# Attention stage of a three-part kernel: another order of the parts of a step, and one rotation of four PSUM banks

## The chip, the cores and the metric

One core of one Trainium2 chip runs the whole program. The metric is the device time of one execution in microseconds (us), the median of several runs.

## The reference

Inputs: q, k, v of 4 batches, 8 heads, 768 positions, 64 channels per head, all float32. Three stages follow one another.

```python
keep = (pos[None, :] < 4) | ((rel >= 0) & (rel < 128))      # 4 sink keys and a window of 128
scores = where(keep, q @ k.T / 8, -1e9); a = softmax(scores); x = a @ v      # heads side by side: 512
theta = x @ w_theta; zr, zi = x * cos(theta), x * sin(theta)
u = x + w_tok_r @ zr + w_tok_i @ zi;  x2 = u + relu(u @ w_ch)
out = (sigmoid(causal_conv5(x2)) * (x2 @ w_val)) @ w_out
```

## The kernel before, in words

The change lies in the first stage, `banded_attention` (L263 to L760). Queries are cut into 24 groups of 128 positions, six to a batch. A query group meets its own 128 keys, the 128 before them and the four sink keys; the first group of a batch has no group before it and no separate sinks, so it has less work. A group has four pairs of heads, and one pair is one step: `for t in range(NT + OT)` (L745) runs 96 steps, and 20 more that drain the pipeline. Several groups are in flight: while step t does the scores of its own pair, it transposes the weights of the pair six steps before, multiplies values of a group ten steps before, and does the theta product of a group twenty steps before.

The order is written out by hand. In each step the loop walks `ORDER` (L21), a list of names. A name is either a part of the step (`parts`, L740), or a queue of postponed pieces of work that `later(kind, steps, f)` filled. What is emitted first stands first in the queue of its engine, and every engine works through its queue strictly in order. `TUNE` (L20) holds the step offsets.

The parts that matter here, for a group g with pairs p0 to p3 (t%4 = 0 to 3):

- `scores` (L418, even steps): TensorE, two pairs at once, into two fixed PSUM tiles `bands` (ps_s, two banks each). A band is free again when `softmax` (L435) of its pair has read it on DVE: `COPY_PREDICATED` L447, then two reductions L449.
- `exp` (ACT L455, then L459): the exponentials with their sums rs. `normalise` (L463, even steps): DVE reciprocal L467, then POOL multiplies a two-pair block (L469) in the next step.
- `turn`, that is `weights_T` (L474, even steps): four transposes on TensorE into ps_t (L480); `tcopy`: ACT copies them out as pc (L484); `cut`: POOL makes the two triangles pp and pc (L491, L493).
- `attend` (L499) and `finish` (L554), at t%4 = 2: 32 (first group: 16) value matmuls L508 into ps_x, then one matmul of the sinks, L558, closes the group; `fcopy` copies ps_x to uT on ACT (L559).
- `sinks` (L517, POOL L524), `sinksT` (L530, TensorE L535 into ps_sk), `scopy` (ACT L541), `slow` (DVE L545), `sink` (POOL L549): they build the operand blk of that sinks' matmul.
- `k`, `q` (L391): transposes of keys and queries for the groups to come (L396), copied by `kcopy` and `qcopy` (L405).
- `split` (ACT L567) and `xl` (POOL L569), `theta` (L574): twelve matmuls L101 to L103 into ps_h; `thcopy` copies them out on ACT (L582).
- `wth`, `range`, `join`, `wturn`, `wcopy`: the weights w_theta, w_tok_r and w_tok_i arrive by DMA (SP's queue) and get rewritten on ACT (L133), POOL (L139) and DVE (L148, L151, L154, L242) between the other work. `keep_warm` (L595) puts idle matmuls into the first steps.

PSUM has eight banks here: four for the bands, one for ps_t, two for ps_m (ps_qk, ps_sk) and one, ps_h, that ps_x, the theta tiles and the warming matmuls share (L269 to L271). In the one bank of ps_h the values of a group can only start when the theta tile ahead of them has been copied out, and theta only when the values ahead of it have been.

After the drain the mixing stage (`mixing`, L843) and the last stage (from L999) follow; neither is edited.

Of the kernel before, what the change touches and what calls it, by code (L numbers as in the profile page):

```python
# [9 lines left out]
F32 = mybir.dt.float32  # L10
# [6 lines left out]
PSUM = bass.MemoryType.PSUM  # L17
DRAM = bass.MemoryType.DRAM

TUNE = dict(tc=0, xs=0, we=0, low=1, cut=1, xl=0, th=0, fx=0, nrm=0, w0=18, ll=8, lv=4, lq=4, lk=5, e=0, l2=0, ws=2, wp=3, ga=0, gc=1, cq=5, ck=5, OT=20, LT=6, OX=10, s1=0, s2=2, sl=1, ss=0, lf=0, rk=0, pcd=0, WP=6, kt=2, bk=3, bq=3, bv=3, bqT=2, first=2, kw=4)  # L20
ORDER = ("range scale warm sinksT cut xl turn scores attend finish wth value wcopy scopy slow tcopy load "  # L21
         "softmax normalise low loads sink exp join sinks k sinkk q split theta qcopy fcopy thcopy fetch kcopy "
         "wturn ").split()

TWO_PI = 6.283185
INV_TWO_PI = 1.0 / (2.0 * math.pi)
# [9 lines left out]
def tile_sink_window_attention__then__token_mix__then__gated_conv(  # L36
# [16 lines left out]
    nc = tc.nc  # L53
    B, H, S, D = q.shape
    P = 128
    NP = H // 2
    NQ = S // P
    DM = H * D
# [24 lines left out]
    wth = [chunks(big.tile([P, KC, DM], F32R, tag=f"wA{z}", name=f"wth{z}")) for z in "hl"]  # L83
    th = {}
# [178 lines left out]
    def banded_attention(mixer):  # L263
        with ExitStack() as c0:
            pa = c0.enter_context(tc.tile_pool(name="pa", bufs=2))
            cq = c0.enter_context(ExitStack())
            pq = cq.enter_context(tc.tile_pool(name="pq", bufs=2, side="right"))
            ps_s = cq.enter_context(tc.tile_pool(name="ps_s", bufs=2, space=PSUM, side="right"))
            ps_t = c0.enter_context(tc.tile_pool(name="ps_t", bufs=1, space=PSUM))  # L269
            ps_m = c0.enter_context(tc.tile_pool(name="ps_m", bufs=2, space=PSUM))  # L270
            ps_h = c0.enter_context(tc.tile_pool(name="ps_h", bufs=1, space=PSUM))  # L271

            ns = max(0, n_sink)
            ns += ns % 2
# [30 lines left out]
            qn, kn, vn, qTs, vss, sms, pTs, sks, blks, xs, pss = ({} for _ in range(11))  # L305
# [85 lines left out]
            def qk_transpose(g, which, p0=0, p1=NP):  # L391
                i = g % NQ
                src = (qn if which == 0 else kn)[g]
                ps = ps_m.tile([P, NP, P], F32, tag="m", name="ps_qk")[:, 0:p1 - p0, :]
                for p in range(p0, p1):
                    nc.tensor.transpose(ps[:, p - p0, :], src[:, 2 * p:2 * p + 2, :].rearrange("s h d -> s (h d)"), ident)  # L396
                if which == 0:
                    if p0 == 0:
                        qTs[g] = pq.tile([P, NP, P], F32, tag="qT", name="qT", bufs=TUNE["bqT"])
                    d = qTs[g][:, p0:p1, :]  # L400
                else:
                    d = kT[:, p0:p1, i, 0:P]

                def copies():
                    copier(which if g == 0 else g < TUNE["ck" if which else "cq"])(d, ps)  # L405
                    if p1 == NP and which == 1 and i == 0 and ns:
# [67 lines left out]
            def weights_T(t):  # L474
                g, p0 = divmod(t, NP)
                i = g % NQ
                sm = sms[g][0]
                ps = ps_t.tile([P, 4, P], F32, tag="t", name="ps_t")
                for n in range(4):
                    nc.tensor.transpose(ps[:, n, :], sm[:, n % 2, p0 + n // 2, ns:], ident)  # L480

                def copy():
                    pc = pa.tile([P, 4, P], F32, tag="pc", name="pc", bufs=3)
                    copier(TUNE['tc'])(pc, ps)  # L484
                    pp = pa.tile([P, 4, P], F32, tag="pp", name="pp", bufs=3) if i > 0 else None
                    pTs[t] = (pc, pp)
                    if i > 0:
                        later("cut", TUNE['cut'], lambda: cut(pc, pp))

                def cut(pc, pp):  # L490
                    nc.gpsimd.affine_select(out=pp, in_=pc, pattern=[[0, 4], [-1, P]], base=0, channel_multiplier=1,  # L491
                                            compare_op=ALU.is_gt, fill=0.0)
                    nc.gpsimd.affine_select(out=pc, in_=pc, pattern=[[0, 4], [1, P]], base=0, channel_multiplier=-1,  # L493
                                            compare_op=ALU.is_ge, fill=0.0)

                later("tcopy", 0, copy)


            def attend(g):  # L499
                i = g % NQ  # L500
                x = xs[g] = ps_h.tile([P, NP, P], F32, tag="h", name="ps_x")
                last = ns == 0 or i == 0
                for p in range(NP):
                    pc, pp = pTs[NP * g + p // 2 * 2]
                    parts = [(g, pc)] if pp is None else [(g, pc), (g - 1, pp)]
                    for a, (gv, w) in enumerate(parts):
                        for h in range(2):
                            nc.tensor.matmul(x[h * D:(h + 1) * D, p, :], vn[gv][:, 2 * p + h, :],  # L508
                                             w[:, p % 2 * 2 + h, :], start=(a == 0 and p == 0),
                                             stop=(last and p == NP - 1 and a == len(parts) - 1),  # L510
                                             skip_group_check=True)
# [18 lines left out]
            def sink_T(g):  # L530
                if ns == 0 or g % NQ == 0:
                    return
                sk = sks.pop(g)
                ps = ps_m.tile([P, NP, P], F32, tag="m", name="ps_sk")[:, 0, :]
                nc.tensor.transpose(ps, sk.rearrange("q a r -> q (a r)"), ident)  # L535
                r = pa.tile([P, P], F32R, tag="skr", name="skr")
                blk = pa.tile([P, NP, P], F32R, tag="blk", name="blk")
                blks[g] = blk

                def copy():  # L540
                    nc.scalar.copy(r, ps)  # L541
                    later("slow", TUNE['sl'], low)

                def low():
                    nc.vector.tensor_tensor(r[64:96, :], ps[64:96, :], r[64:96, :].bitcast(F32), ALU.subtract)  # L545
                    later("sink", TUNE['ss'], block)

                def block():
                    nc.gpsimd.tensor_tensor(blk, r[:, None, :].bitcast(F32).to_broadcast([P, NP, P]),  # L549
                                            bmask[:, :, None].to_broadcast([P, NP, P]), ALU.mult)  # L550

                later("scopy", 0, copy)

            def finish_x(g):  # L554
                b = g // NQ
                x = xs.pop(g)
                if ns and g % NQ:
                    nc.tensor.matmul(x, vss[b], blks.pop(g), start=False, stop=True, skip_group_check=True)  # L558
                later("fcopy", 0, lambda: copier(TUNE['fx'])(uT[:, :, cols(g)], x))  # L559

            def split_x(g):
# [10 lines left out]
            hps = {}  # L572

            def theta(g, c):  # L574
                if c == 0:
                    hps[g] = (ps_m.tile([P, DM], F32, tag="m", name="ps_h") if OT + NP * g > NT - 2 and g % 2 else
                              ps_h.tile([P, DM], F32, tag="h", name="ps_h"))
# [15 lines left out]
            nc.vector.memset(blank, 0.0)  # L593

            def keep_warm(n):  # L595
                warm = ps_h.tile([P, 512], F32, tag="h", name="ps_warm")
# [129 lines left out]
            def step_load_sinks(t, g, p):  # L726
                if ns and g < NG:
# [9 lines left out]
                    if 0 <= n < 6 and b + 1 < B:  # L737
# [398 lines left out]
```

## Time and profile before

| what | value |
|---|---|
| median of 3 runs | 662.92 us (662.25 to 663.28) |
| the profiled execution | 663.22 us; span 661.5 us; mean granted TensorE clock 0.994 |
| busy share of the span | PE 96%, DVE 72%, POOL 60%, ACT 55% |
| attention stage | from 0 to about 235 us, 24 groups; values of group 2 start at 46.89, of group 6 at 84.42, of group 12 at 138.70, of group 18 at 192.97 |
| instructions | 12467 |

The span is counted from the first to the last instruction; the execution's own time is 1.7 us longer. A group of rows by line shows how often an instruction ran, its mean time and what ended the idle time before it; a row of the timeline gives the start, the length and, in brackets, the idle time just before it. Matmuls overlap, so the distance from one start to the next is their price on TensorE, not the length in the row.

### The profile page before, as it was taken

How to read it: one execution, taken by the hardware profiler on the slowest of the kernel's cores; microseconds unless marked ns; L12 is line 12 of the kernel's file. 1: busy time of each engine (PE TensorE's matmuls, PEld its weight loads, DVE VectorE, ACT ScalarE, POOL GpSimd, SP SyncE). 2: the span in 40 equal slices, each digit the busy share in tenths (PEclk: the TensorE clock that was granted, in tenths of full speed). 3: DMA queues.
4: the chain of work that ended last, by engine and by line, in shares of the span. 5: the costliest groups of instructions: out<-in, count | busy, mean ns of one | idle time of the engine just before them, and what ended most of it. 6: DMA issues, size and time to landing. Idle time of an engine off the chain costs nothing.

```text
span 661.5 us, 12467 instructions
## 1 busy us (share of the span) xinstructions
PE 635.8 (96%) x4454; PEld 566.9 (86%) x4454; DVE 477.6 (72%) x1187; ACT 362.1 (55%) x1013; POOL 396.8 (60%) x406
## 2 busy tenths in 40 slices
PE   8679999999999999999999999999999999999998
PEld 4457777777877789999999999999989989989997
DVE  4876677777688449546756767766979889889773
ACT  4779898898898776534353444452423333323222
POOL 4699899879969864324343344447836637537330
PEclk9889999999999999999999999999999999999999
DMA  7686697799982460001000010110010110110111
GB/s 165 162 186 144 139 210 156 147 202 177 199 166 59 137 206 3 1 16 49 33 33 32 33 50 33 49 47 2 1 48 1 49 48 1 49 48 1 49 48 49
DMA packets 104335, 53.36 MB, mean 81 GB/s; under 512 B 80593, under 2 KB 96209, under 8 KB 104273
## 3 DMA queue, kind: packets, MB, share of 16 engines
q1 hardware_dynamic: 104272, 52.56, 32.7%
q8 instruction: 35, 0.57, 0.4%
q14 instruction: 28, 0.22, 0.1%
HBM read 41.54 MB, written 11.01 MB: 79 GB/s over the span
## 4 chain that ended last, share of the span: by engine, by line
PE 69%; POOL 13%; DVE 7%; ACT 5%; issue 3%; DMA 2%; SPq 0%; ACTq 0%; POOLq 0%; DVEq 0%
PE ps_y L103 10%; PE ps_y L101 10%; PE ps_y L102 10%; PE ps_x L508 4%; PE ps_o L103 3%; POOL sm L469 3%; DVE acc L1047 3%; PE ps_o L102 3%; PE ps_o L101 3%; PE ps_c L103 3%; PE ps_c L102 3%; PE ps_c L101 3%; POOL pc L493 2%; PE ps_v L101 2%; PE ps_v L102 2%
## 5 line engine op out<-in xcount | busy, mean ns | idle before, releaser
L98 POOL TENSOR_TENSOR zl<-cs,zh 128x512 fp32r<-128x512 f32 x48 | 65.9, 1373 | 95.2 <-ACT zh L97 80.1
L1047 DVE SCALAR_TENSOR_TENSOR acc<-x,cw,acc 128x384 f32<-128x384 f32 x128 | 106.6, 833 | 2.4
L455 ACT ACTIVATE sm<-sm,nm 128x132 f32<-128x132 f32 (+1 forms) x192 | 76.3, 403 | 13.1 <-DVE nm L449 12.6
L98 POOL TENSOR_TENSOR x2l<-x,x2h 128x384 fp32r<-128x384 f32 x32 | 39.3, 1227 | 55.3 <-ACT x2h L97 55.3
L97 ACT CAST zh<-cs 128x512 fp32r<-128x512 f32 x48 | 29.9, 622 | 76.8 <-DVE cs L892 66.5
L101 PE MATMUL ps_y<-wt0h,zh 128*128 128x384 f32 x192 | 68.2, 355 | 0.0
L469 POOL TENSOR_TENSOR sm<-sm,rs 128x512 f32<-128x512 f32 x48 | 55.9, 1164 | 20.3 <-DVE rs L467 12.7
L103 PE MATMUL ps_y<-wt1h,zl 128*128 128x384 f32 x192 | 64.6, 336 | 0.0
L102 PE MATMUL ps_y<-wt1l,zh 128*128 128x384 f32 x192 | 64.5, 336 | 0.0
L103 PE MATMUL ps_y<-wt0h,zl 128*128 128x384 f32 x192 | 64.5, 336 | 0.0
L102 PE MATMUL ps_y<-wt0l,zh 128*128 128x384 f32 x192 | 64.4, 336 | 0.0
L101 PE MATMUL ps_y<-wt1h,zh 128*128 128x384 f32 x192 | 64.4, 336 | 0.0
L447 DVE COPY_PREDICATED ps_s<-upper,ps_s 128x256 f32<-128x256 int32 x80 | 33.7, 422 | 36.8 <-PE ps_s L432 36.3
L449 DVE CUSTOM_DVE_ANT_0 sm<-ps_s,mask 128x132 f32<-128x132 f32 (+1 forms) x192 | 48.9, 291 | 12.2 <-PE ps_s L424 7.4
L98 POOL TENSOR_TENSOR gl<-acc,gh 128x384 fp32r<-128x384 f32 x28 | 33.7, 1204 | 22.4 <-ACT gh L97 22.4
L508 PE MATMUL ps_x<-pc,vn 128*64 128x128 f32 x384 | 38.0, 286 | 8.8 <-ACT th L582 4.3
L97 ACT CAST x2h<-x 128x384 fp32r<-128x384 f32 x32 | 16.4, 513 | 54.7 <-DVE x L1033 54.7
L101 PE MATMUL ps_v<-x2h,held 128*128 128x384 f32 x128 | 43.3, 338 | 0.0
L102 PE MATMUL ps_v<-x2l,held 128*128 128x384 f32 x128 | 43.2, 338 | 0.0
L103 PE MATMUL ps_v<-x2h,held 128*128 128x384 f32 x128 | 43.2, 338 | 0.0
L892 DVE TENSOR_TENSOR cs<-cs,ps_n 128x512 f32<-128x512 f32 x48 | 32.7, 681 | 11.6 <-ACT cs L885 10.2
L432 PE MATMUL ps_s<-kT,qT 64*64 64x196 f32 x640 | 38.3, 350 | 2.6 <-DVE nm L449 2.2
(159 smaller groups left out, 1937.9 us busy)
## 6 DMA issues: line engine op xcount, KB each, us to landing
vn<-in_v_dram SPq DMA_DIRECT2D x24, 256.0 KB
kn<-in_k_dram SPq DMA_DIRECT2D x23, 256.0 KB
qn<-in_q_dram SPq DMA_DIRECT2D x23, 256.0 KB
out_dram<-o SPq DMA_DIRECT2D x23, 256.0 KB
late<-in_moe_w_tok_r_dram SPq DMA_DIRECT2D x24, 192.0 KB
late<-in_moe_w_tok_i_dram SPq DMA_DIRECT2D x24, 192.0 KB
wTr<-wTe SPq DMA_DIRECT2D x24, 96.0 KB
wTi<-wTe SPq DMA_DIRECT2D x24, 96.0 KB
```

The source lines that it names most:

```text
L97: nc.scalar.copy(dst_h, src)
L98: lo_engine.tensor_tensor(dst_l, src, dst_h.bitcast(F32), ALU.subtract)
L101: nc.tensor.matmul(ps, lhs[0], rhs[0], start=first, stop=False)
L102: nc.tensor.matmul(ps, lhs[0], rhs[1], start=False, stop=False)
L103: nc.tensor.matmul(ps, lhs[1], rhs[0], start=False, stop=last)
L432: nc.tensor.matmul(ps[a:a + QW, h, a:KT + a + QW], qTs[g][d, p, a:a + QW], keys[:, a:KT + a + QW], start=True, stop=True)
L447: nc.vector.copy_predicated(ps[:, :, KT:KT + P], upper.bitcast(I32)[:, None, :].to_broadcast([P, 2, P]), ps[:, :, 0:P])
L449: nc.vector.tensor_tensor_reduce(sm[:, h, p, a:], ps[:, h, P:KT + P - a], m, -SCALE, BIG, ALU.add, ALU.min, nm[:, h, p:p + 1])
L455: nc.scalar.activation(x, x, AF.Exp, bias=nm[:, h, p:p + 1], scale=-1.0, accum_out=rs[:, h, p:p + 1])
L469: later("scale", 0, lambda: nc.gpsimd.tensor_tensor(x, x, r[:, :, :, None].to_broadcast([P, 2, 2, P]), ALU.mult))
L508: nc.tensor.matmul(x[h * D:(h + 1) * D, p, :], vn[gv][:, 2 * p + h, :], w[:, p % 2 * 2 + h, :], start=(a == 0 and p == 0), stop=(last and ...
L1047: nc.vector.scalar_tensor_tensor(a, x2[:, e, z:z + TB], cw[:, e, z:z + 1], a, ALU.mult, ALU.add)
```

## The change

Four edits.

1. `ORDER` is another permutation of the same names. `scores` now stands ahead of `turn` and `attend`; `sinksT` behind `attend`; `tcopy`, `scopy` and `thcopy` ahead of `exp`; `cut` first on POOL; `join` ahead of `normalise`; `wth` and `split` behind `thcopy`; `wcopy` ahead of `load`.
2. Offsets: `s2` 2 to 3 (the sinks' transpose one step later), `lq` 4 to 3 (queries' transposes one step later), `low` 1 to 2, `l2` 0 to 1, `kt` 2 to 4, `cq` 5 to 6 and `ck` 5 to 4 (which of the early q and k copies run on DVE).
3. The sinks' matmul opens the group of the values instead of closing it.
4. The pools ps_t, ps_m and ps_h become one pool of four banks. Every tile that is not of the scores (ps_t, ps_qk, ps_sk, ps_x, ps_h, the warming tile) takes the next bank in turn, so it waits for the readers of the tile four allocations before it.

```diff
-TUNE = dict(tc=0, xs=0, we=0, low=1, ... lq=4, lk=5, e=0, l2=0, ... cq=5, ck=5, ... s2=2, ... kt=2, ...)
-ORDER = ("range scale warm sinksT cut xl turn scores attend finish wth value wcopy scopy slow tcopy load "
-         "softmax normalise low loads sink exp join sinks k sinkk q split theta qcopy fcopy thcopy fetch kcopy "
-         "wturn ").split()
+TUNE = dict(tc=0, xs=0, we=0, low=2, ... lq=3, lk=5, e=0, l2=1, ... cq=6, ck=4, ... s2=3, ... kt=4, ...)
+ORDER = ("warm cut range slow scale xl scores sink turn tcopy attend wcopy sinksT softmax theta load scopy "
+         "finish join normalise k thcopy sinkk wth loads split exp wturn sinks low q fcopy value qcopy kcopy "
+         "fetch").split()
...
-            ps_t = c0.enter_context(tc.tile_pool(name="ps_t", bufs=1, space=PSUM))
-            ps_m = c0.enter_context(tc.tile_pool(name="ps_m", bufs=2, space=PSUM))
-            ps_h = c0.enter_context(tc.tile_pool(name="ps_h", bufs=1, space=PSUM))
+            psum = c0.enter_context(tc.tile_pool(name="psum", bufs=4, space=PSUM))
+
+            def bank(shape, name):
+                return psum.tile(shape, F32, tag="b", name=name)
...
-                x = xs[g] = ps_h.tile([P, NP, P], F32, tag="h", name="ps_x")
-                last = ns == 0 or i == 0
+                x = xs[g] = bank([P, NP, P], "ps_x")
+                sinks = ns > 0 and i > 0
+                if sinks:
+                    nc.tensor.matmul(x, vss[g // NQ], blks.pop(g), start=True, stop=False, skip_group_check=True)
...
-                if ns and g % NQ:
-                    nc.tensor.matmul(x, vss[b], blks.pop(g), start=False, stop=True, skip_group_check=True)
```

How the queues change at the places of which the prediction speaks:

TensorE in the steady state, from the end of a group's theta product to the first value matmuls of the next group's values; ps_s_93 and ps_s_94 are the two bands (ps_s_87 and ps_s_88 in the change). Before:

```order
L103 MATMUL ps_h<-wthh,xl 128x512
L535 MATMUL ps_sk<-ident,sk 128x128
L480 MATMUL ps_t<-ident,sm 128x128 x4
L432 MATMUL ps_s_93<-kT,qT 64x196 x4
L432 MATMUL ps_s_94<-kT,qT 64x196 x4
L508 MATMUL ps_x<-pc,vn 64x128 x2
```

With the change:

```order
L103 MATMUL ps_h<-wthh,xl 128x512
L398 MATMUL ps_qk<-ident,qn 128x128 x4
L434 MATMUL ps_s_87<-kT,qT 64x196 x4
L434 MATMUL ps_s_88<-kT,qT 64x196 x4
L482 MATMUL ps_t<-ident,sm 128x128 x4
L506 MATMUL ps_x<-blk,vr 128x512
L512 MATMUL ps_x<-pc,vn 64x128 x2
```

The queries' transposes came between theta and the scores, the sinks' transpose left this place, the weights' transposes follow the scores, and the sinks' matmul opens the values.

ACT over the same stretch and on to the copy of ps_x. Before:

```order
L567 CAST xh<-uT 128x512
L405 COPY qT<-ps_qk 128x512
L455 ACTIVATE sm,rs<-sm,nm 128x132 x2
L459 ACTIVATE rs<-rs,eps 128x2x2
L582 COPY th_791<-ps_h 128x512
L541 CAST skr<-ps_sk 128x128
L484 COPY pc<-ps_t 128x512
L455 ACTIVATE sm,rs<-sm,nm 128x132 x2
L559 COPY uT<-ps_x 128x4x128
```

With the change:

```order
L568 CAST xh<-uT 128x512
L457 ACTIVATE sm,rs<-sm,nm 128x132 x2
L582 COPY th_774<-ps_h 128x512
L457 ACTIVATE sm,rs<-sm,nm 128x132 x2
L461 ACTIVATE rs<-rs,eps 128x2x2
L407 COPY qT<-ps_qk 128x512
L486 COPY pc<-ps_t 128x512
L457 ACTIVATE sm,rs<-sm,nm 128x132 x2
L560 COPY uT<-ps_x 128x4x128
L545 CAST skr<-ps_sk 128x128
```

The copy of the theta tile moved ahead of the exponentials of the same step, the copy of the queries behind them, and the sinks' copy behind that of ps_x.

TensorE in the start-up, around the transposes of the second group's sinks. Before:

```order
L598 MATMUL ps_warm<-blank 128x512
L535 MATMUL ps_sk<-ident,sk 128x128
L480 MATMUL ps_t<-ident,sm 128x128 x4
L432 MATMUL ps_s_93<-kT,qT 64x196 x4
L432 MATMUL ps_s_94<-kT,qT 64x196 x4
L508 MATMUL ps_x<-pc,vn 64x128 x8
```

With the change:

```order
L434 MATMUL ps_s_87<-kT,qT 64x196 x4
L434 MATMUL ps_s_88<-kT,qT 64x196 x4
L482 MATMUL ps_t<-ident,sm 128x128 x4
L512 MATMUL ps_x<-pc,vn 64x128 x8
L539 MATMUL ps_sk<-ident,sk 128x128
L398 MATMUL ps_qk<-ident,kn 128x128 x4
```

The sinks' transpose stood ahead of the weights' transposes, the scores and the values of its step, and now stands behind all three.

## Rows read from the trace of the kernel before

**Rows 1.** Busy time by stretch: us, then each engine, granted clock, DMA

```profile
84.42:138.70 54.28, 51.67 (x530) 40.67 (x530) 40.24 (x157) 48.34 (x163) 48.01 (x53) 1.00 0.85 175
...
232.72:661.50 428.78, 424.83 (x2383) 406.66 (x2383) 313.50 (x560) 170.15 (x369) 201.80 (x168) 1.00 0.11 38
```

**Rows 2.** Waits of TensorE, 47 to 240 us: total, times, longest

```profile
PE ps_x L508 <- ACT th L582: 4.3, 9, 0.9
PE ps_x L508 <- issue: 2.2, 2, 1.2
PE ps_x L508 <- POOL xl L569: 1.9, 2, 0.9
```

**Rows 3.** Waits of TensorE, 0 to 47 us

```profile
PE ps_sk L535 <- POOL sk L524: 5.4, 3, 2.2
...
PE ps_t L480 <- ACT pc L484: 1.4, 1, 1.4
```

**Rows 4.** Timeline of TensorE: start, length, instruction, idle time before it

```profile
102.47 0.39 PE L508 MATMUL ps_x<-pc,vn 128*64 128x128 f32 x4
102.69 0.39 PE L508 MATMUL ps_x<-pp,vn 128*64 128x128 f32 x4
103.00 0.50 PE L558 MATMUL ps_x<-blk,vr 128*128 128x512 f32 x1
103.34 0.60 PE L396 MATMUL ps_qk<-ident,kn 128*128 128x128 f32 x4
103.78 0.60 PE L480 MATMUL ps_t<-ident,sm 128*128 128x128 f32 x4
...
108.53 0.40 PE L103 MATMUL ps_h<-wthh,xl 128*128 128x512 f32 x1
...
108.87 0.60 PE L480 MATMUL ps_t<-ident,sm 128*128 128x128 f32 x4
109.40 0.89 PE L432 MATMUL ps_s<-kT,qT 64*64 64x196 f32 x16
111.23 0.44 PE L508 MATMUL ps_x<-pc,vn 128*64 128x128 f32 x4 [0.94 <-ACT th L582]
...
122.92 0.89 PE L432 MATMUL ps_s<-kT,qT 64*64 64x196 f32 x16
123.74 0.65 PE L396 MATMUL ps_qk<-ident,qn 128*128 128x128 f32 x4
```

**Rows 5.** Timeline of ACT, the same group

```profile
109.48 0.42 ACT L455 ACTIVATE sm<-sm,nm 128x132 f32<-128x132 f32 x1
...
110.61 0.57 ACT L582 COPY th<-ps_h 128x512 f32<-128x512 f32 x1
```

**Rows 6.** Timeline of DVE, three places

```profile
101.91 1.68 DVE L154 SCALAR_TENSOR_TENSOR wc<-late,wc 128x768 int32<-128x768 int32 x1
...
110.03 0.43 DVE L447 COPY_PREDICATED ps_s<-upper,ps_s 128x256 f32<-128x256 int32 x1 [2.11 <-PE ps_s L432]
...
111.02 1.10 DVE L148 TENSOR_SCALAR wc<-wc 128x768 int32<-128x768 int32 x1
...
127.72 1.75 DVE L151 SCALAR_TENSOR_TENSOR wc<-late,wc 128x768 int32<-128x768 int32 x1
```

**Rows 7.** Timeline of POOL in the start-up

```profile
23.91 1.27 POOL L98 TENSOR_TENSOR wthl<-wc,wthh 128x512 fp32r<-128x512 f32 x1 [2.03 <-ACT wthh L97]
...
29.30 1.33 POOL L469 TENSOR_TENSOR sm<-sm,rs 128x512 f32<-128x512 f32 x1 [1.41 <-DVE rs L467]
...
42.23 1.27 POOL L98 TENSOR_TENSOR wthl<-wc,wthh 128x512 fp32r<-128x512 f32 x1 [1.23 <-ACT wthh L97]
...
47.59 1.28 POOL L569 TENSOR_TENSOR xl<-uT,xh 128x512 fp32r<-128x512 f32 x1
```

**Rows 8.** Waits of POOL, 84 to 193 us

```profile
POOL sm L469 <- DVE rs L467: 6.4, 4, 1.9
POOL sk L524 <- DVE rs L467: 4.5, 2, 2.3
```

More of the change, by code (lines that the diff above doesn't have):

```diff
@@ L18 @@
 DRAM = bass.MemoryType.DRAM
-TUNE = dict(tc=0, xs=0, we=0, low=1, cut=1, xl=0, th=0, fx=0, nrm=0, w0=18, ll=8, lv=4, lq=4, lk=5, e=0, l2=0, ws=2, wp=3, ga=0, gc=1, cq=5, ck=5, OT=20, LT=6, OX=10, s1=0, s2=2, sl=1, ss=0, lf=0, rk=0, pcd=0, WP=6, kt=2, bk=3, bq=3, bv=3, bqT=2, first=2, kw=4)
-ORDER = ("range scale warm sinksT cut xl turn scores attend finish wth value wcopy scopy slow tcopy load "
-         "softmax normalise low loads sink exp join sinks k sinkk q split theta qcopy fcopy thcopy fetch kcopy "
-         "wturn ").split()
+TUNE = dict(tc=0, xs=0, we=0, low=2, cut=1, xl=0, th=0, fx=0, nrm=0, w0=18, ll=8, lv=4, lq=3, lk=5, e=0, l2=1, ws=2, wp=3, ga=0, gc=1, cq=6, ck=4, OT=20, LT=6, OX=10, s1=0, s2=3, sl=1, ss=0, lf=0, rk=0, pcd=0, WP=6, kt=4, bk=3, bq=3, bv=3, bqT=2, first=2, kw=4)
+ORDER = ("warm cut range slow scale xl scores sink turn tcopy attend wcopy sinksT softmax theta load scopy "
+         "finish join normalise k thcopy sinkk wth loads split exp wturn sinks low q fcopy value qcopy kcopy "
+         "fetch").split()
 TWO_PI = 6.283185
@@ L393, in qk_transpose @@
                 src = (qn if which == 0 else kn)[g]
-                ps = ps_m.tile([P, NP, P], F32, tag="m", name="ps_qk")[:, 0:p1 - p0, :]
+                ps = bank([P, NP, P], "ps_qk")[:, 0:p1 - p0, :]
                 for p in range(p0, p1):
@@ L477, in weights_T @@
                 sm = sms[g][0]
-                ps = ps_t.tile([P, 4, P], F32, tag="t", name="ps_t")
+                ps = bank([P, 4, P], "ps_t")
                 for n in range(4):
@@ L508, in attend @@
                             nc.tensor.matmul(x[h * D:(h + 1) * D, p, :], vn[gv][:, 2 * p + h, :],
-                                             w[:, p % 2 * 2 + h, :], start=(a == 0 and p == 0),
-                                             stop=(last and p == NP - 1 and a == len(parts) - 1),
+                                             w[:, p % 2 * 2 + h, :], start=(not sinks and a == 0 and p == 0),
+                                             stop=(p == NP - 1 and a == len(parts) - 1),
                                              skip_group_check=True)
@@ L533, in sink_T @@
                 sk = sks.pop(g)
-                ps = ps_m.tile([P, NP, P], F32, tag="m", name="ps_sk")[:, 0, :]
+                ps = bank([P, NP, P], "ps_sk")[:, 0, :]
                 nc.tensor.transpose(ps, sk.rearrange("q a r -> q (a r)"), ident)
@@ L554, in finish_x @@
             def finish_x(g):
-                b = g // NQ
                 x = xs.pop(g)
-                if ns and g % NQ:
-                    nc.tensor.matmul(x, vss[b], blks.pop(g), start=False, stop=True, skip_group_check=True)
                 later("fcopy", 0, lambda: copier(TUNE['fx'])(uT[:, :, cols(g)], x))
@@ L575, in theta @@
                 if c == 0:
-                    hps[g] = (ps_m.tile([P, DM], F32, tag="m", name="ps_h") if OT + NP * g > NT - 2 and g % 2 else
-                              ps_h.tile([P, DM], F32, tag="h", name="ps_h"))
+                    hps[g] = bank([P, DM], "ps_h")
                 x2 = xs[g, "hl"]
@@ L595, in keep_warm @@
             def keep_warm(n):
-                warm = ps_h.tile([P, 512], F32, tag="h", name="ps_warm")
+                warm = bank([P, 512], "ps_warm")
                 for _ in range(n):
```

## The prediction

> **What bounds the kernel now.** I read the busy time by stretch first, to see which engine each stage is full of. From group 6 to group 12, one batch, TensorE is busy 51.67 of 54.28 us [rows 1]; POOL has 48.01 and ACT 48.34, so they have 6 us of room in a batch and TensorE 2.6. From 232.72 us to the end TensorE is busy 424.83 of 428.78 us [rows 1]: nothing in the change touches that stretch, and I leave it as it is. What can be won lies in TensorE's waits of the first 235 us, and the second view lists them.
>
> From 47 to 240 us thirteen waits stand at one instruction, the first value matmul: 4.3 us released by the theta copy on ACT, 2.2 with no releaser and 1.9 put down to POOL, 8.4 together [rows 2]. Two timelines show why. The last theta matmul starts at 108.53, transposes and scores follow at 108.87 and 109.40, and the values start at 111.23, behind an idle 0.94 [rows 4]. ACT was doing the exponentials of p1 from 109.48 and came to the theta copy only at 110.61; it took 0.57 and ended 0.05 before the values started [rows 5]. Values and theta share one bank, and the copy that frees it stands behind exponentials. That a part of the 8.4 us has another name I put down to the same bank, since it is the same instruction with the same length of wait; if not, the 4.3 us are the lower end.
>
> In the first 47 us TensorE waits 5.4 us in three waits for POOL's sinks' weights, with transposes and scores queued behind, and 1.4 us for the single ps_t bank [rows 3].
>
> **The change part by part.** The sum is made against the profiled execution of 663.2 us, which lies 0.3 above the median shown.
>
> *Banks in turn, theta's copy ahead of the exponentials.* A steady group now takes seven tiles in this order: transposes, theta, queries, transposes, values, sinks, keys. Four back from the values lies the first transposes' tile, copied long before; theta's tile is now awaited by the sinks' transpose, 4 us of TensorE work later. So all thirteen waits go: -8.4 us (at least -4.3). In exchange theta waits for the copy of ps_x, as it did before. ACT, in order, now stands idle at the theta copy until theta ends, about 1 us a group. That costs nothing as long as ACT has room: 54.28 less 48.34 is 5.9 us a batch, 1.0 a group [rows 1]. If it had none, the exponentials would be late, then the reciprocal, then POOL; their results are wanted only one to two steps later.
>
> *Order on TensorE.* No instruction is added or removed. By distances from start to start the price of most blocks stays: scores followed by transposes 0.82 (122.92 to 123.74), four transposes 0.44 (103.34 to 103.78), the sinks' matmul 0.34 (103.00 to 103.34) [rows 4]. Where the array's shape changes (the third field, 128\*64, 64\*64, 128\*128) there is an extra: 0.53 instead of 0.44 for transposes ahead of scores (108.87 to 109.40), 0.31 instead of 0.22 from the last values to the sinks (102.69 to 103.00) [rows 4]. A full group had five such changes and now has six, because scores sit between two blocks of transposes and the sinks' matmul no longer follows the values. The price is 0.09 in 20 groups, +1.8 us; the ends are 0 (the block left may have paid it already) and 3.2 (0.50 of the sinks' length less its 0.34 distance, the whole overlap lost, 20 times [rows 4]). The Trainium skill, TensorEngine Tiling (Array Packing), section Key Properties, says that changing the tiling mode drains TensorE, which speaks against an order with one more change; by it the term would be the upper end and the time 1.4 us longer, and the 0.09 of the rows shows much less than an empty engine.
>
> *Scores first.* A band is filled again sooner. From the scores of p2 and p3 to the second half of the next scores TensorE has 0.82 + 0.44 + 0.34 + 1.85 (seven distances of 0.22 and one 0.31) + 0.11 (one transpose, a quarter of 0.44) + 0.53 + 0.41 (the first half of the scores) = 4.50 us of work. DVE needs 0.63 until it starts (109.40 to 110.03), 0.99 for softmax and reciprocal (to 111.02), a piece of the weights' work of 1.10, and 0.90 for the second softmax (0.99 less a short reciprocal): 3.62; with a piece of 1.68 it is 4.20 [rows 4, 6]. Both fit, with 0.3 us to spare. They don't where DVE comes late: behind a piece of 1.75 in the step before [rows 6] I reckon 0.7 late, and 0.4 us of wait. The weights' jobs come every one and a half groups and every second one has its pieces in those steps: 6 groups, +2.4 us, between 0 and the rival below.
>
> *Start-up.* The three waits for the sinks' weights no longer hold up scores, since the sinks' transpose stands behind them and a step later; the copy of ps_t no longer waits for a weights' piece whose DMA is late, and has another bank anyhow. The most is 5.4 + 1.4 = 6.8 us [rows 3]. What is late next is POOL: from 23.91 to 47.59 it is idle only 1.41 + 1.23 = 2.6 us [rows 7]. So the stretch can shrink by that, plus what the first of these rows starts earlier; it waited 2.03 for ACT, and I take 1.6 of it. Together -4.2 us, ends 0 and -6.8.
>
> *With no price of their own.* The sinks' matmul is only moved, but now needs blk at the start of the values instead of the end; blk is made two steps ahead, so TensorE's 3 us of earlier work cover it. `cut` first and `join` ahead of the reciprocal change when POOL waits, not how much it does; what that could cost is the first rival. Of the early copies one goes from ACT to DVE and one back. On SP the stores of the turned weights go ahead of a step's loads; loads are issued eight steps before use, so a store that waits some 2 us for DVE stays hidden.
>
> The sum: -8.4 + 1.8 + 2.4 - 4.2 = -8.4, hence 654.8 against the profiled execution and 654.5 us as a median.
>
> **The rivals.** *POOL becomes the bound.* In two batches POOL waits 6.4 + 4.5 us for the reciprocal [rows 8], 5.5 a batch; with its 48.01 of work that is 53.5 of 54.28. If these waits stay, and they may, because up to 1.75 us of weights' work now stands ahead of the reciprocal, a batch shrinks by 0.8 only. Three batches give -2.4, the start-up nothing: 660.5. For it: POOL has the least room after TensorE. Against: those waits are there because POOL had caught up with a slower TensorE, and shrink as it is asked for more. Chance 0.14.
>
> *The wait moves to theta.* Theta still needs the copy of ps_x, and from the last value matmul to theta TensorE now has 0.11 + 0.53 + 0.82 + 0.44 = 1.9 us of work where it had 0.34 + 0.44 + 0.53 + 0.82 + 0.41 = 2.5. If ACT is behind by 1.4 us there (the copy itself is 0.5), the bank wait is back under another name: -8.4 falls away, the other terms cancel, and the time is 663. For it: ACT is the most filled after TensorE and POOL in rows 1. Against: in the new order it idles for theta once in each group, which absorbs lateness. Chance 0.10.
>
> *The bands become the bound, and it is slower.* If DVE needs not 4.20 but 5.3 us between the two scores, because pieces of 1.7 us stand in both steps, every group loses 0.8 at the scores: 20 times, +16 in place of +2.4, and 668. The turning point is 0.54 us a group (10.8 us over 20 groups), that is 5.04 us on DVE against the 4.50 that TensorE leaves. For it: the pieces reach 1.68 and 1.75 [rows 6]. Against: DVE has 14 us of room in a batch [rows 1], and the sinks' small correction left that interval. Chance 0.12.
>
> **How the numbers follow.** The forecast has 0.64. The lower end of the range, 648.5, is the forecast with terms two and three at nothing and 6 us from the start-up; the upper, 662, takes in the POOL case and half of what the bands may add. About 0.06 lies below and 0.14 above. A measurement of this kernel can tell about 0.2%, 1.3 us. Faster by more: the forecast, most of the POOL case (0.11) and 0.02 of theta's, 0.77. Within: 0.03 and 0.06, 0.09. Slower: the bands and 0.02 of theta's case, 0.14.
>
> **What would show it.** Right: no wait at the first value matmul or at the sinks' opening one; a batch near 51.5 to 52.5 us between the same values of groups 6 and 12; the values of group 2 (46.9 us before) some 4 us earlier; ACT idle ahead of the theta copy, released by TensorE. Each step is wrong if its sign is missing: waits of theta's first matmul for the copy of ps_x, waits of the scores for DVE of more than 0.4 us in most groups, or waits for POOL ahead of the transposes or in the values. The whole is wrong if the stretch after the attention stage changes its length by more than 1 us.

## The result and the profile after

| | median | spread | ratio to the kernel before, 95% interval |
|---|---|---|---|
| before | 662.66 us | 662.25 to 663.28, 4 runs | |
| with the change | 653.52 us | 653.26 to 654.30, 4 runs | 0.9863 (0.9846 to 0.9880) |

The change is faster by 9.1 us, 1.4%. The profiled executions give 661.5 and 652.0 us of span, 9.5 less. The prediction was 654.5 in a range of 648.5 to 662.

By stretch, in the changed kernel (us, then each engine's busy time, granted clock, DMA); the cuts are the first value matmuls of groups 3, 6, 12 and 18 and the first `ps_y` matmul of the mixing stage:

```profile
55.55:82.29 26.74, 26.20 (x266) 20.43 (x265) 19.36 (x74) 24.12 (x82) 25.05 (x27) 1.00 0.70 145
82.29:134.27 51.98, 51.98 (x532) 40.35 (x531) 38.51 (x155) 48.21 (x163) 48.90 (x53) 1.00 0.89 184
...
186.25:234.17 47.92, 47.79 (x438) 37.64 (x437) 31.34 (x102) 39.63 (x116) 43.05 (x46) 1.00 0.57 153
234.17:652.00 417.83, 413.88 (x2313) 397.59 (x2311) 308.16 (x554) 163.65 (x357) 194.39 (x164) 1.00 0.09 32
```

The same stretches that [rows 1] don't have, of the kernel before:

```profile
56.28:84.42 28.14, 26.54 (x265) 20.74 (x265) 19.60 (x76) 24.02 (x82) 24.54 (x26) 1.00 0.73 151
192.97:243.70 50.73, 48.12 (x435) 37.84 (x436) 32.24 (x104) 39.31 (x115) 42.98 (x45) 1.00 0.52 143
243.70:661.50 417.80, 413.85 (x2313) 397.62 (x2311) 308.35 (x554) 163.61 (x357) 194.65 (x165) 1.00 0.09 32
```

A batch took 54.28 us and takes 51.98, and now TensorE is busy in all of it. Up to group 6 the kernel is 2.13 us ahead, each of two batches adds 2.3, the end of the attention stage 2.81, and the untouched rest differs by 0.03.

TensorE's waits from 47 to 240 us, all that are left of the 9.7 that stood there (thirteen at the values, [rows 2], and 1.3 us of others):

```profile
PE ps_s L434 <- DVE nm L451: 0.5, 1, 0.5
```

And in the first 47 us, where [rows 3] stood before:

```profile
PE ps_s L434 <- DVE nm L451: 5.9, 5, 3.5
...
PE ps_x L506 <- POOL blk L553: 0.5, 1, 0.5
```

The waits for the sinks' weights are gone; in their place the scores wait for DVE, 5.9 us in five pieces, where one such wait of 1.5 us stood before. A full group in the middle of the stage shows the dense case (TensorE, then ACT). It answers to [rows 4, 5]:

```profile
105.68 0.40 PE L103 MATMUL ps_h<-wthh,xl 128*128 128x512 f32 x1
105.92 0.60 PE L398 MATMUL ps_qk<-ident,qn 128*128 128x128 f32 x4
106.45 0.90 PE L434 MATMUL ps_s<-kT,qT 64*64 64x196 f32 x16
107.27 0.66 PE L482 MATMUL ps_t<-ident,sm 128*128 128x128 f32 x4
107.69 0.48 PE L506 MATMUL ps_x<-blk,vr 128*128 128x512 f32 x1
108.10 0.44 PE L512 MATMUL ps_x<-pc,vn 128*64 128x128 f32 x4
```

```profile
106.12 0.59 ACT L582 COPY th<-ps_h 128x512 f32<-128x512 f32 x1
106.60 0.41 ACT L457 ACTIVATE sm<-sm,nm 128x132 f32<-128x132 f32 x1
```

No row has an idle time in brackets. Theta's copy starts 0.44 after the start of theta's last matmul and is done at 106.71, a microsecond before the values' group opens. ACT now stands and waits for theta, and for the values (its waits from 84 to 193 us):

```profile
ACT th L582 <- PE ps_h L103: 3.9, 9, 0.6
ACT uT L560 <- PE ps_x L512: 3.0, 6, 0.6
```

### The profile page after: what moved, and what is told of

Its sections match the earlier page's. It is cut to its first block, busy times and chain, and to the rows that moved or that the text cites. A ratio compares the mean times of both kernels' runs of the same rounds, so it can differ in the third digit from the quotient of the medians.

```text
span 652.0 us, 12510 instructions
## 1 busy us (share of the span) xinstructions
PE 636.7 (98%) x4452; PEld 565.5 (87%) x4454; DVE 471.3 (72%) x1187; ACT 362.1 (56%) x1013; POOL 398.5 (61%) x406
## 4 chain that ended last, share of the span: by engine, by line
PE 79%; POOL 8%; DVE 7%; issue 2%; DMA 2%; SPq 1%; ACT 1%; DVEq 0%; POOLq 0%
PE ps_y L103 10%; PE ps_y L101 10%; PE ps_y L102 10%; PE ps_x L512 4%; PE ps_s L434 4%; PE ps_o L103 3%; DVE acc L1047 3%; PE ps_o L101 3%; PE ps_o L102 3%; PE ps_t L482 3%; PE ps_h L102 3%; PE ps_h L103 3%; PE ps_h L101 3%; PE ps_c L101 3%; PE ps_c L103 3%; PE ps_c L102 3%
## 5 line engine op out<-in xcount | busy, mean ns | idle before, releaser
L471 POOL TENSOR_TENSOR sm<-sm,rs 128x512 f32<-128x512 f32 x48 | 53.8, 1120 | 8.9 <-DVE rs L469 8.9
L892 DVE TENSOR_TENSOR cs<-cs,ps_n 128x512 f32<-128x512 f32 x48 | 32.7, 682 | 10.9 <-ACT cs L885 10.9
L101 PE MATMUL ps_h<-wthh,xh 128*128 128x512 f32 x96 | 39.8, 415 | 0.0
```

Of the source, the lines that this page charges most:

```text
L101: nc.tensor.matmul(ps, lhs[0], rhs[0], start=first, stop=False)
L471: later("scale", 0, lambda: nc.gpsimd.tensor_tensor(x, x, r[:, :, :, None].to_broadcast([P, 2, 2, P]), ALU.mult))
L892: nc.vector.tensor_tensor(x, x, pn[:, None, :].to_broadcast([P, 2, HD]), ALU.mult)
```

## The experiments

Each was run beside the kernel before on the same chip, in five rounds. "g3" to "g18" is the start of the values of that group in the profile, "mix" the first matmul of the mixing stage. Before and after stand there for comparison. The kernel before took 663.2 to 663.3 us in these runs and 662.7 beside the changed kernel, so medians of the two sets can be compared to about 0.6 us.

| kernel | median us | ratio (95%) | g3 | g6 | g12 | g18 | mix | span |
|---|---|---|---|---|---|---|---|---|
| before | 662.66 | | 56.28 | 84.42 | 138.70 | 192.97 | 243.70 | 661.5 |
| changed | 653.52 | 0.985 to 0.988 | 55.55 | 82.29 | 134.27 | 186.25 | 234.17 | 652.0 |
| rot_only | 656.94 | 0.989 to 0.992 | 56.05 | 81.93 | 134.42 | 186.90 | 237.06 | 654.9 |
| order_only | 656.23 | 0.988 to 0.991 | 53.99 | 81.87 | 133.93 | 186.01 | 236.59 | 654.4 |
| old_pools | 656.23 | 0.989 to 0.992 | 55.64 | 81.99 | 133.97 | 185.96 | 236.26 | 654.1 |
| theta_copy_only | 674.01 | 1.015 to 1.018 | 56.05 | 86.10 | 144.22 | 202.55 | 254.27 | 672.1 |
| exp_behind | 665.00 | 1.002 to 1.004 | 57.86 | 85.04 | 139.12 | 192.80 | 245.25 | 663.0 |
| five_changes | 652.11 | 0.982 to 0.985 | 53.16 | 80.48 | 132.32 | 184.12 | 232.81 | 650.6 |
| sinks_last | 653.57 | 0.984 to 0.987 | 52.98 | 80.87 | 132.92 | 184.99 | 233.26 | 651.0 |
| weights_later | 655.46 | 0.987 to 0.990 | 56.48 | 83.83 | 135.81 | 187.79 | 235.71 | 653.5 |
| sinks_turn_early | 658.00 | 0.991 to 0.995 | 60.20 | 86.40 | 138.86 | 191.32 | 240.44 | 658.3 |
| double_fold | 672.69 | 1.014 to 1.016 | 60.94 | 89.00 | 146.13 | 203.26 | 254.53 | 672.3 |
| fetch_early | 650.77 | 0.980 to 0.983 | 51.17 | 79.04 | 130.99 | 182.95 | 230.85 | 648.6 |
| five_fetch | 650.66 | 0.980 to 0.983 | 51.36 | 78.68 | 130.52 | 182.35 | 231.03 | 648.8 |

### Which edit takes the waits at the values away

**rot_only**, the kernel before with the rotation of four banks and nothing else:

```diff
-            ps_t, ps_m, ps_h: pools of 1, 2 and 1 bank
+            psum = c0.enter_context(tc.tile_pool(name="psum", bufs=4, space=PSUM))
```

> The kernel before with the fourth edit alone: one rotation of four banks, the old order of a step, the sinks' matmul last. Theory (the bank is the cause, and the rotation cures it): the values' bank is the one of the queries' transposes, copied long before, so the thirteen waits at the values go (8.4 us) and there is no added change of the array's shape: 653 to 655 us. Rival (the place of theta's copy behind the exponentials is the cause, whatever the bank): the waits stay or move to the next tile, 660 to 663 us.

**order_only**, the new `ORDER` and `TUNE` (edits 1 and 2) with the old pools and the sinks' matmul last:

> The new order and offsets alone (edits 1 and 2), the old pools, the sinks' matmul last. Theory (the order alone takes the waits at the values away, 1.8 us of TensorE work cover theta's copy): 653 to 656 us. Rival (theta and values in one bank: what was waited for at the values is waited for at theta, which has 1.9 us for the copy of ps_x): 658 to 663 us, with waits of L101 for the copy of ps_x.

**old_pools**, the changed kernel with edit 4 undone:

> The changed kernel with the fourth edit undone: three pools again, the new order, the sinks' matmul first. If the rotation is needed, waits come back at theta or at the sinks' matmul that opens the values: 657 to 663 us. If the order alone did it: within 1.5 us of the changed kernel, 652 to 655 us.

Either half does it: the waits for theta's copy are gone in the middle of the stage in all three runs. The rotation alone takes a batch from 54.28 to 52.49 us, the order alone to 52.06, and the new order with the old pools and with the sinks' matmul first to 51.98, the changed kernel's own length. So in the middle of the stage the rotation adds nothing to the order. All three medians lie above what was expected of a cure (655, 656 and 655 us at most); a wait in rot_only and the end of the stage, both below, are why. The Trainium skill, Perfetto Trace Analysis, section Matmuls, says that independent groups should rotate through PSUM banks so that the copy of one overlaps the matmuls of the next; rot_only agrees (6 us), and order_only shows that another order, in which the copy stands ahead of the exponentials, does the same with one bank. In rot_only TensorE has new waits, all at the first transposes of keys in a batch; the profile puts two of them down to ACT (first row) and one to the keys' transfer (second row):

```profile
PE ps_qk L398 <- ACT sm L457: 1.9, 2, 1.2
PE ps_qk L398 <- DMA kn<-in_k_dram: 1.2, 1, 1.2
```

All three look like the transfer. Theta's copy, which frees the bank that these transposes take next, was done at 135.20, a microsecond before the transposes at 136.26 (SP's queue, ACT and TensorE in rot_only), and likewise at 187.68 before those at 189.15. The keys' transfer had gone out at 130.50 and 182.99, 5.8 and 6.2 us before TensorE went on, against 5.7 (78.50 to 84.17) for the wait that bears its name:

```profile
130.50 0.58 SPq L365 DMA_DIRECT2D kn<-in_k_dram  x1
```

```profile
134.63 0.57 ACT L583 COPY th<-ps_h 128x512 f32<-128x512 f32 x1
```

```profile
136.26 0.63 PE L398 MATMUL ps_qk<-ident,kn 128*128 128x128 f32 x4 [0.75 <-ACT sm L457]
```

What the two edits do only together lies at the end of the stage. From group 18 to the mixing stage the old pools need 50.3 to 50.6 us, the rotation with the old order 50.16, both together 47.92. With the old pools the last group's values still wait for theta in the one bank. Scores have run out, so TensorE has no other work between them, and theta's copy comes late because ACT does cosines of the mixing stage first, with 1.28 us for a table (TensorE, then ACT in old_pools):

```profile
225.16 0.47 PE L503 MATMUL ps_x<-blk,vr 128*128 128x512 f32 x1 [1.92 <-ACT th L580]
```

```profile
222.43 1.28 ACT L882 ACT_TABLE_LOAD   x1
...
224.45 0.56 ACT L580 COPY th<-ps_h 128x512 f32<-128x512 f32 x1
```

In order_only the same wait, 1.88 at 225.60, is listed with no releaser.

**theta_copy_only** and **exp_behind**, both the kernel before with one name of the order moved:

```diff
-         "... normalise low loads sink exp join sinks k sinkk q split theta qcopy fcopy thcopy fetch kcopy "
+theta_copy_only: "... normalise low loads sink thcopy exp join sinks k sinkk q split theta qcopy fcopy fetch kcopy "
+exp_behind:      "... normalise low loads sink join sinks k sinkk q split theta qcopy fcopy thcopy exp fetch kcopy "
```

> The kernel before with one name of the order moved: theta's copy ahead of the exponentials on ACT; the old pools. Theory (either half of the step is enough): theta ends near 108.9 in the group of rows 4, the copy takes 0.57 and is done before TensorE has finished transposes and scores (110.3), so the waits at the values go: 654 to 656 us. Rival (exponentials behind an idle ACT are late and hold something else, or only the rotation cures it): 659 to 664 us.

The edit did the opposite of what its expectation says. `theta` stands behind in the walk, so a queue of copies that is emptied before it finds nothing, and the copy goes out a step later. The waits grew, which makes the run a test from the other side: the later the copy, the longer the values wait, 21.6 us in these two rows (the first two of TensorE's waits from 47 us on).

```profile
PE ps_x L508 <- ACT th L582: 16.1, 16, 1.5
PE ps_x L508 <- issue: 5.5, 4, 1.4
```

> The kernel before with one name of the order moved, this time the exponentials: behind theta's copy of the same step; old pools, TensorE's order as before. Theory (theta's copy stood behind exponentials, and one bank joins theta and values): the copy ends 0.6 after theta and TensorE has 1.4 us of transposes and scores in between, so the waits at the values go, without an added change of the array's shape: 653 to 656 us. Rival (exponentials that come last on ACT delay the reciprocal, and POOL or the transposes wait): 658 to 666 us.

Here the copy does come before the exponentials, and the waits at the values for theta's bank shrink to 1.2 us at the last group and 0.2 at another; one for POOL's triangles pc grew from 0.4 to 1.0. Yet nothing is won, 665.0 us. TensorE's waits from 47 us on:

```profile
PE ps_qk L396 <- DMA kn<-in_k_dram: 3.2, 3, 1.3
PE ps_s L432 <- DVE nm L449: 3.0, 5, 0.7
PE ps_x L508 <- issue: 1.2, 1, 1.2
PE ps_x L508 <- POOL pc L493: 1.0, 1, 1.0
```

and in the start-up those for the sinks' weights grew from 5.4 to 7.2 us. The rival was right that the cost moves, though not to POOL alone: the batch is back at 54.08 us with other names at the waits. Taking one wait away was not enough; the order as a whole took its successors away too. In this run the keys' transfer goes out at 82.11, behind four weight loads, and TensorE stands for it until 87.44, as in rot_only. In the changed kernel it goes out at 77.83 and its transposes start at 83.48 without a wait, hardly later; no run tests what keeps the new order clear of it.

### What the shape changes and the third edit cost

**five_changes** and **sinks_last**:

```diff
-ORDER = ("... xl scores sink turn tcopy attend wcopy ... load scopy finish join ...")
+sinks_last:   "... xl scores sink turn tcopy attend finish wcopy ... load scopy join ..."   and the sinks' matmul in finish_x, as before
+five_changes: "... xl sink turn scores tcopy attend finish wcopy ... load scopy join ..."   and the same
```

> The changed kernel with the scores behind the weights' transposes again and the sinks' matmul last: five changes of the array's shape in a full group in place of six; offsets, rotation and ACT's order as changed. Theory (a change of shape costs 0.09 to 0.11, all of it on the path): 20 groups by that, 1.8 to 2.2 us less than the changed kernel, 651.3 to 652.0 us, and a batch of about 51.4 us. Rival (the scores have to go first, or DVE or the values wait): 653.5 to 657 us with waits of the scores for DVE.

> The changed kernel with the third edit undone: the sinks' matmul closes the values again. Theory (six changes of shape either way, and the operand has time enough): 653.0 to 654.5 us, a batch of 52.0. Rival (opening the values with a whole-bank matmul is what saved time): 655 to 657 us.

Full groups without any wait last 8.89 and 8.90 us in the changed kernel (values at 90.31, 99.20, 108.10) and 8.83 and 8.82 in five_changes (88.15, 96.98, 105.80): one change of the array's shape less is worth 0.07 us a group. The batch shrinks by 0.14 only, since some scores stall on DVE (0.16 at 123.11). The 1.4 us by which the median is lower come from the start-up, 1.8 at group 6, less 0.8 that the end gives back. sinks_last shows the same start-up gain (group 3 2.6 us sooner) without the lower number of changes, keeps 1.4 of it at group 6 and 0.9 at the mixing stage, and its median equals the changed kernel's. In neither run is this gain a wait less. Up to group 3 TensorE is idle for 10.97 us in five_changes and 10.60 in sinks_last, and for 10.70 in the changed kernel; it is busy for 42.19 and 42.38 in place of 44.85, at a mean granted clock of 0.94 and 0.97 in place of 0.91. So edit 3 by itself is worth nothing that these runs can tell.

The Trainium skill, TensorEngine Tiling (Array Packing), section Key Properties, says that a change of mode drains TensorE; 0.07 us for one more change is less than half of the 0.16 of lost overlap that the prediction's upper end put on it.

### What keeps the start-up long

**sinks_turn_early**: in the changed kernel `s2` is 2 again and `sinksT` stands ahead of `scores`.

> The changed kernel with the sinks' transpose back ahead of the scores and a step sooner (offset s2 3 to 2), as it stood before. The prediction's start-up term: the three waits for POOL's sinks' weights come back and hold the scores up, 3 to 5 us, 656.5 to 658.5 us, the values of group 6 at 85 to 87. Rival, which the changed kernel's trace speaks for (its start-up waits 5.9 us for DVE instead, and group 6 began only 2.1 us sooner, as much as the three bank waits before it had been): the start-up is set by w_theta's transfers and the work on them, and the place of the transpose is worth under 1.5 us: 653.5 to 655 us.

**weights_later**: `ws` 2 to 3.

> The changed kernel with the first weights' work one step later (offset ws 2 to 3). In the changed kernel's start-up ACT waits 2.78 us for the DMA of w_theta in front of exponentials, DVE behind them, and TensorE's scores 3.46 us for DVE. Theory (that DMA in ACT's queue is what keeps the start-up long): the scores at 24.5 come 1.5 to 3 us sooner, 650.5 to 652 us. Rival (the start-up waits for something else next, POOL or the DMA itself): 653 to 655 us.

The first says that the start-up term's cause is real: with the transpose back in its place TensorE waits again, and longer than in [rows 3], group 6 starts 4.1 us later and the median is 4.5 higher (the profiled execution, 659.98 us, lies 2.0 above that median):

```profile
PE ps_sk L537 <- POOL sk L526: 10.4, 3, 5.1
```

But the changed kernel's start-up had hardly become shorter, so something else took the place. Its trace tells what (rows of ACT, DVE, TensorE and SP's queue in the changed kernel):

```profile
20.50 0.67 ACT L133 ACTIVATE wc<-late 128x512 f32<-128x512 f32 x1 [2.78 <-DMA late<-in_moe_w_theta_dram]
```

```profile
22.16 0.28 DVE L390 TENSOR_TENSOR vr<-vs,vr 32x128 fp32r<-32x128 f32 x1 [2.34 <-ACT vr L389]
```

```profile
24.53 1.94 PE L434 MATMUL ps_s<-kT,qT 64*64 64x196 f32 x16 [3.46 <-DVE nm L451]
```

```profile
10.02 4.19 SPq L384 DMA_DIRECT2D vs<-in_v_dram  x6
...
15.36 0.87 SPq L120 DMA_DIRECT2D late<-in_moe_w_theta_dram  x1
```

ACT waits for the second piece of w_theta, and since its queue is strict, the exponentials and the cast `vr` stand behind; DVE waits for `vr`, with the copy of keys and the softmax behind it; the softmax is what frees the band. weights_later didn't help (655.5): the transfer goes out at 15.48, as late as in the changed kernel, so ACT still waits 1.65 us until 20.24, and later 3.35 us for POOL's part of the weights. It doesn't test the theory, and the next run moves the fetch alone.

**fetch_early**, and **five_fetch** (the same in five_changes):

```diff
-                    if t >= TUNE['ws'] + TUNE['wp'] * c and wstages[c]:
+                    at = TUNE['ws'] + TUNE['wp'] * c
+                    early = c == 1 and t == at - 2
+                    if early or (t > at if c == 1 else t >= at) and wstages[c]:
```

> The changed kernel with the second piece of w_theta fetched at step 3 instead of 5, ahead of the six small loads of the sinks' values on SP; its later work stays where it is. In the changed kernel that fetch goes out at 15.36 us, while the transfers were at 0.15 of their share from 12 to 16 us, and ACT stands 2.78 us at 20.5 for it with exponentials behind. Theory (this one transfer keeps the start-up long): the 3.46 us wait of the scores shrinks by 2 to 3, the drop of the granted clock behind it with it, and the time is 649.5 to 652 us. Rival (POOL and DVE are next in the start-up, or the groups to follow are fed too late): 652.5 to 654.5 us.

> The same earlier fetch in the kernel with five changes of the array's shape (scores behind the weights' transposes, sinks' matmul last), which took 652.11 us. If the two gains add: 648 to 650.5 us. If the start-up has another bound: 651.5 to 652.5 us.

One transfer sent two steps sooner makes the kernel 2.7 us faster by the medians. The fetch goes out at 9.38, ACT takes the piece up at 17.27 without a wait, and the scores stand 1.32 us instead of 3.46 (SP's queue, ACT, TensorE in fetch_early):

```profile
9.38 0.94 SPq L120 DMA_DIRECT2D late<-in_moe_w_theta_dram  x1
```

```profile
17.27 0.69 ACT L133 ACTIVATE wc<-late 128x512 f32<-128x512 f32 x1
```

```profile
22.18 0.56 PE L434 MATMUL ps_s<-kT,qT 64*64 64x196 f32 x8 [1.32 <-DVE nm L451]
```

Group 3 starts 4.4 us sooner, group 6 3.3, and the 3.3 last to the mixing stage. But the 4.4 us are not a sum of waits. Up to group 3 TensorE is idle for 10.70 us in the changed kernel and for 10.76 here, since other waits took the long one's place (in the first 47 us those for keys' transfers grew from 1.0 to 1.9, for instance). What shrinks is its busy time, 44.85 to 40.41 for the same work, with the granted clock at 1.00 in place of 0.91 (stretches up to group 3 in the kernel before, the changed one and fetch_early; a row that stalls counts as busy):

```profile
0.00:56.28 56.28, 43.95 (x384) 29.28 (x384) 36.99 (x150) 38.48 (x137) 38.77 (x67) 0.94 0.73 165
```

```profile
0.00:55.55 55.55, 44.85 (x382) 29.19 (x384) 35.55 (x151) 38.27 (x136) 38.32 (x66) 0.91 0.79 172
```

```profile
0.00:51.17 51.17, 40.41 (x382) 25.71 (x384) 35.45 (x151) 38.02 (x136) 37.71 (x65) 1.00 0.86 184
```

So what the earlier fetch bought shows as clock: the stretch at half clock that follows the long wait in the changed kernel is not there. That the wait caused the fall is not shown; order_only waits 3.7 us at its longest and has 0.97 up to group 3.

The gains of five_changes and of the earlier fetch don't add. The values of group 6 start at 80.48 with the first, at 79.04 with the second and at 78.68 with both, and five_fetch gives back at the end what it has ahead; its median lies between its two expected ranges. 650.8 and 650.7 us, which are equal within their intervals, are the fastest versions here, 12 us under the kernel before.

### How close the bands are

**double_fold**:

```diff
-                    nc.vector.copy_predicated(ps[:, :, KT:KT + P], ...)
+                    for _ in range(2):
+                        nc.vector.copy_predicated(ps[:, :, KT:KT + P], ...)
```

> The changed kernel with the masked copy on the band (L449) done twice for every pair, the second time over the same numbers: 0.44 us more on DVE for each of a step's pairs, 0.88 between two scores, 160 pairs in all. Theory of the bands (between two scores TensorE leaves DVE 4.5 us; the closest step of the trace has 0.29 us to spare, others 0.75 to 1.2): the closest steps, about six to thirteen, lose 0.6 each, the rest little, 3 to 8 us slower than the changed kernel with waits of the scores for DVE. Rival (DVE, idle 13 of 52 us in a batch, swallows it): under 1.5 us slower.

(The copy runs for the 80 pairs that have a group before them, not for 160.) The loss is 19.2 us, over twice what I expected at most, and it turns the gain into a loss. A batch, and TensorE's and DVE's waits in two batches, 89 to 203 us:

```profile
89.00:146.13 57.13, 53.19 (x531) 39.94 (x530) 49.67 (x175) 48.73 (x163) 45.29 (x53) 1.00 0.82 167
```

```profile
PE ps_s L434 <- DVE nm L452: 7.6, 10, 1.2
```

```profile
DVE skr L550 <- ACT skr L546: 5.4, 4, 2.2
DVE ps_s L450 <- PE ps_s L434: 3.7, 4, 1.1
```

DVE is busy 49.67 of 57.13 us: not full, but of its 13.5 idle us in a batch of the changed kernel only a part was to be had. In two of its batches it waits 9.8 us for scores and 7.5 for ACT's copy of the sinks:

```profile
DVE ps_s L449 <- PE ps_s L434: 9.8, 10, 1.7
DVE skr L549 <- ACT skr L545: 7.5, 4, 2.2
```

The first shrank to 3.7 as DVE filled up; the second is an engine standing in front of its own work, and 5.4 of it stay. So the rival of the bands is a real edge close by, which this change doesn't step over.

## Why the prediction was right

The time, 9.5 us less in the profile where 8.4 was forecast, and the main mechanism came out as forecast. Two of the four terms were mis-sized, by 2.9 us one way and 4.0 the other, and mostly cancel; that the total came out so close is luck in that part.

- **Banks and theta's copy, -8.4: right.** The waits at the values that made it up are gone. From group 3 to the mixing stage TensorE's idle time fell from 1.60 + 2.61 + 2.59 + 2.61 = 9.41 us to 0.54 + 0 + 0 + 0.13 = 0.67. What was listed with no releaser and under POOL did belong to the same bank: it went with the rest. What the text did not see is that the order alone would have done this in the batches, and that the rotation pays at the last groups, where ACT's cosines hold theta's copy up. ACT's idle time at theta's copy came to 3.9 us in two batches, where the text took about 1 us a group.
- **Order on TensorE, +1.8: nearly right.** 0.07 a group in place of 0.09, measured against five_changes, hence 1.4 us in 20 groups, an estimate. (That five_changes is also 1.4 us faster is no proof of it, as said there.) Against a full group of the kernel before without a wait in it, 8.79 us (92.32 to 101.11), it is 0.10 to 0.11, hence 2.1.
- **Scores first, +2.4: wrong, about -0.5.** Six groups were to wait 0.4 for DVE. Before, two waits (0.7) and two rows of scores of 1.23 us in place of 0.89 stood there, together 1.4; after, one wait of 0.5 and two rows of 1.1, together 0.9. The two fences behind this list show them. I took the place and the length of the weights' pieces over from the old order, although the change moves `join` ahead of `normalise`; that is the step that failed. The 0.7 us late were reckoned behind a piece of 1.75; from 47 us on the longest of these pieces lasts 1.54 in the changed kernel. The edge was right, as double_fold shows.
- **Start-up, -4.2: wrong, about -0.2.** Group 6 starts 2.13 us sooner, and 0.54 + 0.99 + 0.44 = 1.97 of that are the bank waits at groups 3, 5 and 6. The step that failed is "What is late next is POOL". Late next was one transfer of w_theta in ACT's queue, seen by TensorE two engines later as a wait for DVE. Up to group 3 TensorE's idle time fell by 1.63 us only (12.33 to 10.70, and 0.54 of that is the bank), and its busy time grew by 0.90 (43.95 to 44.85) at a lower granted clock, for which the sum had no term. The sign that I had named, group 2 some 4 us sooner, gave 1.44 (46.89 to 45.45). sinks_turn_early shows that the three waits had to go; in fetch_early, where the long wait and the falls of the clock are gone, group 2 does start 5.0 us sooner (41.93).
- **The remainder.** These four give -8.4 + 1.4 - 0.5 - 0.2 = -7.7. Waits of 0.43 and 0.24 at the end of the stage, which I had not counted, went too. The last 1.1 us (1.8 with the higher price of a change of shape) I can't divide; 0.67 of it is less busy time in the first and last of the stretches (26.54 to 26.20, 48.12 to 47.79). By stretch nothing is left over: 0.73 us up to group 3, 8.74 of idle and 0.06 of busy time from there to the mixing stage, less 0.03 behind it, are the 9.5.
- **The rivals.** POOL did not become the bound: it is busy 48.90 of 51.98, and its waits for the reciprocal fell from 10.9 [rows 8] to 2.3, as argued; 2.6 us of waits for ACT's copy pc are new. Theta's first matmul nowhere waits for the copy of ps_x. The bands hold. With no price of their own: the sinks' matmul first does wait once, 0.5 for blk in the start-up, where the text saw it covered; after 47 us none of TensorE's waits is for a load, so the stores on SP stayed hidden. (`wcopy` stood ahead of `load` in the old order too, so these stores are no change.)

TensorE's timeline of the kernel before, and of the changed one; a row of scores without a stall has 0.89:

```profile
104.31 1.23 PE L432 MATMUL ps_s<-kT,qT 64*64 64x196 f32 x16
...
213.52 0.56 PE L432 MATMUL ps_s<-kT,qT 64*64 64x196 f32 x8 [0.54 <-DVE nm L449]
```

```profile
72.42 0.56 PE L434 MATMUL ps_s<-kT,qT 64*64 64x196 f32 x8 [0.54 <-DVE nm L451]
...
123.87 1.09 PE L434 MATMUL ps_s<-kT,qT 64*64 64x196 f32 x16
```

## What to carry to other kernels

A tile that waits for its bank can be cured at either end: by another bank, or by bringing the copy that frees it forward in its engine's queue. Test each alone, since they need not add, and look at the ends of a pipeline, where the work that covers a wait runs out. When a wait is taken away, follow what is behind it through the strict queues to its first cause, here three engines back at a DMA's place in SP's queue. Then set idle and busy time apart, since what the next step gains can be clock and not waiting. And an engine's idle time is room only as far as it does not wait there for a third one.

## What the runs showed of the hardware

The granted clock in the start-up differs between kernels of the same work, and costs microseconds. After the 3.46 us wait the changed kernel's TensorE runs at 0.51, close to the lower of its two levels (1.2 of 2.4 GHz), and again at 0.57 after 40 to 44 us, in which it was busy 2.91 of 4 and never idle for more than 1.00 at a time; a row of four value matmuls there takes 0.64 instead of 0.39 us (changed kernel, stretches; the first holds the long wait):

```profile
20.00:24.00 4.00, 1.02 (x8) 0.75 (x7) 1.60 (x4) 3.47 (x13) 0.61 (x1) 1.00 0.85 211
24.00:28.00 4.00, 3.39 (x26) 1.88 (x28) 3.85 (x19) 3.23 (x12) 3.54 (x5) 0.51 0.08 21
44.00:48.00 4.00, 3.47 (x27) 2.84 (x27) 2.16 (x12) 2.21 (x9) 3.93 (x6) 0.57 1.28 223
```

fetch_early, whose longest wait there is shorter, has 1.00 in all of these and a mean of 1.000 over the span, and its lead at group 3 is busy time, as shown above. At 0.91 over 55.55 us the changed kernel lacks 5.0 us of clock, an estimate of the most that this can explain; 4.4 came back. five_changes was busy only 2.64 of 4 us from 40 to 44 and kept 1.00 behind it, so busy time in a stretch alone does not tell when the clock falls.

Six loads of 4 KB each took 4.19 us of SP's queue (10.02 to 14.21), while the transfers stood at 0.45 of their share, and at 0.06 from 12 us on. The Trainium skill, Perfetto Trace Analysis, section What "DMA-bound" means, counts the issuing engine's sequencer as a bound of its own; here it was that for 4 us, and the load that mattered stood behind.
